# Second MLP of an attention kernel: weights cross DRAM unsplit and are split where they are used

## The chip, the cores and the metric

One core of one Trainium2 chip runs the whole kernel in one launch. The metric is device time in microseconds (us). The engines are TensorE (PE, matmul; PEld is its weight load), VectorE (DVE), ScalarE (ACT), GpSimd (POOL) and SyncE (SP). DMA transfers are issued from the instruction streams of SP and ACT.

## The reference

Linear attention, then two MLPs, each of two layers; 4 x 576 = 2304 tokens, model width 512, hidden width 2048. The weights of the MLPs come as float64, the other inputs and the output as float32.

```python
def phi(x):
    proj = einsum('bhsd,df->bhsf', x, w_phi)
    proj = proj - max(abs(proj), axis=-1)
    return concat([exp(proj), exp(-proj)])
q_p, k_p = phi(q), phi(k)
kv, z = einsum('bhsf,bhsd->bhfd', k_p, v), sum(k_p, axis=2)
x = einsum('bhsf,bhfd->bhsd', q_p, kv) / (einsum('bhsf,bhf->bhs', q_p, z) + 1e-6)
x = x as (2304, 512)
h = x @ moe_w_in;  x = maximum(0.01 * h, h) @ moe_w_out        # first MLP
h = x @ moe2_w_in; out = (h * tanh(softplus(h))) @ moe2_w_out  # second MLP
```

## The kernel before, in words

**Products.** A float32 operand is split in a high part (fp32r, a copy on ACT, `high`) and a low part (the rest, a subtraction on DVE, `low`), and a product is three matmuls: high x high, high x low, low x high (`three`, L95 to L97). Both MLPs work in 2 x 2 blocks with seven products instead of eight. For this each pair f of 128-wide blocks of the hidden width (f = 0 to 7) has seven left operands, A11, A12, A22 and the sums S1 to S4. For the first weights these lie in four parts of a pair: part 0 holds A11 and A12, part 1 A22, part 2 S3 and S1, part 3 S2 and S4. Part 1 is 256 words wide per high or low, the others 512.

**Stages.** The attention comes first, then for each MLP a first layer (`first`: 16 items, one per pair f and half sb of the tokens, and 8 smaller items for the 256 left-over tokens) and a second layer. The first MLP's second layer is `emit_y` in 72 steps. In the second MLP's first layer an item's results leave PSUM by Mish on ACT (`mish`, L1378), differences are formed on DVE (L1402), and seven tiles of 256 KB per item are stored in DRAM (gp<-g, L1376). The second MLP's second layer is `emit_s`: per half 28 steps (7 products x 4 groups of two pairs, fp = 0 to 3), each with 12 matmuls; its inputs are loaded again as 512 KB (raw<-gp, L1430) by `Halves.load` and split (L91, L92) by `Halves.splits`; then 8 steps for the left-over tokens.

**Weights.** A 128-wide block of weights is a unit (MLP, block, 0 for first or 1 for second weights). Its float64 words are loaded (stage<-in_..., 512 KB) and converted (`conversion`, L159) to 128 x 512 float32 words: clamp, shift, sign and mask on DVE, a scale on ACT, a join on DVE. All conversions of the second MLP's weights run during the first MLP. Then:

- First weights, `w2_chain(f)` (L1026), for all eight pairs: the converted words are split in the four parts, the sums formed between, and the split parts stored (pd<-wp). In the second MLP's first layer `load_w2(f, i)` (L1340) loads part i of pair f, 512 or 256 KB in all, straight into the place from which PE reads, when `two_.after` says that pair f-2 is done with that place.
- Second weights: `to_store` writes the converted words (scr<-c). In the second MLP's first layer `o2_chain(f)` (L1275) fetches two units (c<-scr), splits and sums them in the tiles wq ("v4" to "v7"), reordering the columns on the way (`mixed`, `plain`), and stores each of seven operands as high and low (qd<-wq, 256 KB). `to_home(n)` (L1326) loads two pairs of an operand (wo<-qd, 512 KB) into the home from which PE reads, 28 homes in all: 8 behind the gate "s0", 6 behind "s1", 14 behind "c1". These open two steps into the first layer's last cycle, two steps behind that cycle, and at the layer's end.

**Order.** The streams of all engines are written out by hand: `cycle(n)` emits the products of an item (the products that end an item stand in the next item's cycle), and calls `work()` between products, seven times a cycle. `work` advances chains of stages (`Stage`, `Chain`, `Lane`, from L670 on): a queue in order, at most four chains active, the head of the queue not passed by a later one; a stage waits for its gate in `free`, for `after` steps since the stage before, and for tokens that bound DVE's work. `need(mark)` calls `work(True)`, which ignores step counts and tokens, until a stage with that mark is done. `later(n, f)` emits f n steps on. Each DMA of `o2_chain`, `load_w2` and `to_home` is issued by SP, each gp<-g and raw<-gp by ACT.

**Words.** `Places` hands out tiles of 128 x 512 words for converted or fetched weights (`take`, `drop`), the longest unused first. In the second MLP's first layer three are left.

Of the kernel before, what the change touches and what calls it, by code (L numbers as in the profile page):

```python
# [20 lines left out]
def attention_two_mlps_kernel(  # L21
# [17 lines left out]
    P = 128  # L39
# [119 lines left out]
    def conversion(u, then, early=False):  # L159

        box = {}

        def low_bits():
            stg = box["s"]
            e = box["e"] = places.take(places.words) if early else stg[:, :, 0]
            nc.vector.scalar_tensor_tensor(out=e.bitcast(I32) if early else e, in0=stg[:, :, 1], scalar=-(1 << 31),
                                           in1=stg[:, :, 0], op0=ALU.bitwise_and, op1=ALU.bitwise_or)
            if early:
                loaded()
# [5 lines left out]
        def clamp():  # L175
# [3 lines left out]
            nc.vector.tensor_scalar(out=c, in0=stg[:, :, 1].bitcast(F32), scalar1=F64_TOP, scalar2=-F64_TOP,  # L179
                                    op0=ALU.min, op1=ALU.max)  # L180
            nc.vector.tensor_scalar(out=stg[:, :, 0], in0=stg[:, :, 0], scalar1=29, scalar2=None,
# [105 lines left out]
    with tc.manual_schedule():  # L287
# [976 lines left out]
        TO = ((A11,), (A12, A22), (S2, S3), (S4, S1))  # L1264
        qd, home2 = {}, {}

        def mixed(t, *h):

            hs = slice(2 * h[0], 2 * h[0] + 2) if h else slice(0, 4)
            return t.rearrange("p (i x e) -> p x i e", i=KD, x=KD)[:, hs]  # L1270

        def plain(t):
            return t.rearrange("p (x i e) -> p x i e", i=KD, e=P // KD)

        def o2_chain(f):  # L1275
            c, part = [], {}
# [4 lines left out]

            def sums(*todo):
                (l0, r0), (l1, r1) = ([x.rearrange("p (i h y) -> p h i y", i=KD, h=2)[:, h] for h in range(2)] for x in c)
# [4 lines left out]
            def views(i):  # L1288
                if i not in part:
                    part[i] = place("v%d" % (4 + i), F32R, 2, DM, name="wq")  # L1290
                src = mixed(c[i % 2], 0) if i == 0 else mixed(c[i % 2])
                n = E if i == 0 else 2 * E
                return [plain(part[i][:, x, 0:n]) for x in range(2)] + [src]

            def hi(i):
                return lambda: high(views(i))

            def lo(i):
                def put():
                    for x, o in enumerate(TO[i]):  # L1300
                        if (o, f // 2) not in qd:
                            qd[o, f // 2] = dr.tile([P, 2, 2, E], F32, name="qd%d_%d" % (o, f // 2))
                        nc.sync.dma_start(out=qd[o, f // 2][:, f % 2], in_=part[i][:, :, x * E:(x + 1) * E].bitcast(F32))
                return lambda: (low(views(i)), later(2, put))
# [375 lines left out]
```

## Time and profile before

| | |
|---|---|
| time, three runs | 948.32, 949.54, 949.75 us; median 949.54 |
| profiled execution | 947.93 us, span 945.8 us |
| PE busy | 903.7 us (96%) |
| DVE, ACT busy | 626.7 us (66%), 503.6 us (53%) |
| mean granted PE clock | 0.981 of full |
| moved by DMA | 231.88 MB, 245 GB/s over the span |
| chain that ended last | PE 80%, DMA 14%, DVE 3% |

The span runs from the first to the last instruction; the time holds some 2 us around it. The first MLP's first layer begins near 175 us, its second layer near 346, the second MLP's first layer at 543 and its second at 749. A releaser (`<-`) is inferred: it is what ended an engine's idle time.

### The profile page before, as it was taken

To read this page: it belongs to the slowest core of one execution; us is meant where nothing else is said; L and a number is where in the kernel's file an instruction comes from. 1 tells how busy PE (TensorE), PEld (TensorE's weight loads), DVE (VectorE), ACT (ScalarE), POOL (GpSimd) and SP (SyncE) were. 2 spreads that over 40 slices of the span, in tenths; PEclk is the share of its full clock that TensorE was granted. 3 is DMA by queue.
4 is the path that set the end of the run, shared out by engine and by line. 5 is a ranking of instruction groups with operands and counts; after the bars stand their busy time and mean duration, and the time that the engine had idled before them with its cause. 6 is when DMAs were issued, how large, how long until landed. Compare 5 with 4: busy or idle time off the path is not lost.

```text
span 945.8 us, 17104 instructions
## 1 busy us (share of the span) xinstructions
PE 903.7 (96%) x6549; PEld 772.2 (82%) x6549; DVE 626.7 (66%) x1055; ACT 503.6 (53%) x827; POOL 68.7 (7%) x36
## 2 busy tenths in 40 slices
PE   8999999999999999999999998988999569999998
PEld 7999999788888888889888887776778448888887
DVE  7999988588889437888898266545553235654551
ACT  6898898565566554545555264433442234444441
POOL 4435333000000000000000000000000000000000
PEclk9999999999999999999999999998999779999999
DMA  7535420369888777899974639999999996786772
GB/s 208 140 80 159 125 71 8 119 220 327 277 287 268 257 259 248 316 345 328 311 266 153 205 120 315 384 374 367 344 374 367 415 415 219 216 242 209 213 196 59
DMA packets 159554, 231.88 MB, mean 245 GB/s; under 512 B 51569, under 2 KB 91633, under 8 KB 159473
## 3 DMA queue, kind: packets, MB, share of 16 engines
q1 hardware_dynamic: 110336, 127.50, 41.3%
q10 hardware_dynamic: 49136, 103.31, 31.4%
q8 instruction: 51, 0.84, 0.4%
q14 instruction: 31, 0.25, 0.1%
HBM read 136.90 MB, written 93.85 MB: 244 GB/s over the span
## 4 chain that ended last, share of the span: by engine, by line
PE 80%; DMA 14%; DVE 3%; ACT 1%; issue 1%; ACTq 1%; POOL 0%; SPq 0%; DVEq 0%
PE a L95 13%; PE a L96 12%; PE a L97 12%; PE b L95 11%; PE b L96 11%; PE b L97 11%; DMA gp<-g 5%; DMA qd<-wq 4%; PE outs L479 3%; PE kvp L456 3%; DMA w<-pd 2%; DMA wo<-qd 2%; PE a L372 1%; PE xt L504 1%; DMA raw<-gp 1%; PE kvp L459 1%
## 5 line engine op out<-in xcount | busy, mean ns | idle before, releaser
L92 DVE TENSOR_TENSOR g<-raw,g 128x1024 fp32r<-128x1024 f32 (+1 forms) x64 | 76.1, 1189 | 87.2 <-ACT g L91 87.1
L91 ACT ACTIVATE g<-raw 128x1024 fp32r<-128x1024 f32 (+1 forms) x64 | 66.1, 1032 | 94.1 <-PE b L97 40.4
L92 DVE TENSOR_TENSOR gl<-raw,gh 128x512 fp32r<-128x512 f32 x72 | 49.7, 690 | 43.4 <-ACT gh L91 41.5
L91 ACT ACTIVATE gh<-raw 128x512 fp32r<-128x512 f32 x72 | 45.1, 628 | 61.0 <-PE b L97 17.9
L439 POOL PARTITION_ALL_REDUCE qm<-qd x32 | 68.5, 2188 | 86.0 <-ACT qd L434 77.2
L95 PE MATMUL b<-win,w 128*128 128x512 f32 x128 | 51.8, 405 | 18.9 <-ACT b L780 11.1
L96 PE MATMUL b<-gl,wo 128*128 128x512 f32 (+1 forms) x192 | 67.9, 354 | 0.0
L95 PE MATMUL b<-gh,wo 128*128 128x512 f32 (+1 forms) x192 | 67.9, 354 | 0.0
L97 PE MATMUL b<-gh,wo 128*128 128x512 f32 (+1 forms) x192 | 67.9, 354 | 0.0
L1402 DVE TENSOR_TENSOR g<-g,g 128x512 f32<-128x512 f32 x32 | 22.1, 690 | 44.3 <-ACT g L1382 44.0
L96 PE MATMUL b<-win,w 128*128 128x512 f32 x128 | 50.9, 398 | 0.0
L97 PE MATMUL b<-win,w 128*128 128x512 f32 x128 | 50.8, 397 | 0.0
L95 PE MATMUL a<-gh,wo 128*128 128x512 f32 x128 | 49.8, 389 | 0.0
L96 PE MATMUL a<-gl,wo 128*128 128x512 f32 x128 | 49.8, 389 | 0.0
L97 PE MATMUL a<-gh,wo 128*128 128x512 f32 x128 | 49.8, 389 | 0.0
L95 PE MATMUL b<-g,wo 128*128 128x512 f32 x128 | 49.8, 389 | 0.0
L96 PE MATMUL b<-g,wo 128*128 128x512 f32 x128 | 49.8, 389 | 0.0
L97 PE MATMUL b<-g,wo 128*128 128x512 f32 x128 | 49.8, 389 | 0.0
L95 PE MATMUL a<-g,wo 128*128 128x512 f32 x96 | 39.4, 410 | 9.9 <-ACT g L91 9.9
L95 PEld LDWEIGHTS b<-win,w 128*128 128x128 f32 x128 | 24.7, 193 | 26.5 <-ACT b L780 13.7
L830 DVE TENSOR_TENSOR g<-b,z 128x512 f32<-128x512 f32 x31 | 21.3, 689 | 30.6 <-PE b L97 30.1
L95 PE MATMUL a<-win,w 128*128 128x512 f32 x96 | 38.4, 400 | 2.5 <-DMA w<-pd 2.5
(280 smaller groups left out, 2601.0 us busy)
## 6 DMA issues: line engine op xcount, KB each, us to landing
gp<-g ACTq DMA_DIRECT2D x112, 256.0 KB, 5.2
raw<-gp ACTq DMA_DIRECT2D x56, 512.0 KB, 4.3
raw<-gd ACTq DMA_DIRECT2D x72, 256.0 KB, 3.7
gd<-g ACTq DMA_DIRECT2D x71, 256.0 KB, 3.5
stage<-in_moe_w_in_dram SPq DMA_DIRECT2D x32, 512.0 KB, 5.2
stage<-in_moe_w_out_dram SPq DMA_DIRECT2D x32, 512.0 KB, 5.0
qd<-wq SPq DMA_DIRECT2D x56, 256.0 KB, 5.4
wo<-qd SPq DMA_DIRECT2D x28, 512.0 KB, 7.7
```

The lines of the kernel that those rows point to most:

```text
L91: nc.scalar.activation(out=hi, in_=src, func=AF.Copy)
L92: nc.vector.tensor_tensor(out=lo, in0=src, in1=hi.bitcast(F32), op=ALU.subtract)
L95: nc.tensor.matmul(out=o, lhsT=wh_, rhs=xh, start=start, stop=False, **kw)
L96: nc.tensor.matmul(out=o, lhsT=wh_, rhs=xl, start=False, stop=False, **kw)
L97: nc.tensor.matmul(out=o, lhsT=wl_, rhs=xh, start=False, stop=stop, **kw)
L372: nc.tensor.transpose(out=t[:, j * P:(j + 1) * P], in_=s[nm + "n"].rearrange("p h t d -> p (h t d)")[:, j * P:(j + 1) * P], identity=ident)
L439: nc.gpsimd.partition_all_reduce(qm, qd, P, bass_isa.ReduceOp.absmax)
L456: nc.tensor.matmul(out=both[r, h, a, :], lhsT=s["kp"][a][:, h, t, r], rhs=s["vm"][:, h, t, :], start=(a == 0 and h == 0 and t == 0), stop= ...
L459: nc.tensor.matmul(out=both[r, :, a, :], lhsT=l["lp"][a][:, i % 2, r], rhs=s["vl"], start=False, stop=(a == 1), skip_group_check=True)
L479: nc.tensor.matmul(out=g[r, u // 2, u % 2, h], lhsT=s["qp"][a][:, h, q0 + r.start:q0 + r.stop], rhs=s["kv"][:, 2 * h + a], start=(a == 0), ...
L830: nc.vector.tensor_tensor(out=c, in0=x["Y"], in1=cur[0].z7[n % 2], op=ALU.add)
L1402: nc.vector.tensor_tensor(out=out_, in0=in0, in1=in1, op=ALU.subtract)
```

## The change

The second MLP's weights cross DRAM in another form. (1) `conversion`: units of the second MLP's second weights are permuted as they are converted (`mixed`, `flat`), so that later readers find the columns in order. (2) Only pairs 0 and 1 of the first weights go through `w2_chain`; the units of pairs 2 to 7 are stored as plain words. (3) `late_chain(f)` fetches the two units of such a pair in the second MLP's first layer and splits them into the places of `load_w2`, part by part, as pair f-2 leaves them. (4) `o2_chain` stores A11, A12 and A22 straight from the fetched words, forms the sums and stores them, unsplit: 128 KB each. (5) `to_home` loads 256 KB into one of six tiles ("a0" to "a5") and splits them into the home. (6) The two stage tiles "st0" and "st1" give four more words in this stage.

```diff
 def conversion(u, then, early=False):
+        turned = bool(u[0] and u[2])
+        mixed = lambda t: t.rearrange("p (x i e) -> p i x e", x=KD, i=KD)
+        flat = lambda t: t.rearrange("p (i x e) -> p i x e", x=KD, i=KD)
         def low_bits():
+            if turned:
+                nc.vector.tensor_scalar(out=mixed(e.bitcast(I32)), in0=flat(stg[:, :, 0]), scalar1=29, scalar2=None,
+                                        op0=ALU.logical_shift_right)
+                nc.vector.scalar_tensor_tensor(out=e.bitcast(I32), in0=box["c"].bitcast(I32), scalar=-(1 << 31),
+                                               in1=e.bitcast(I32), op0=ALU.bitwise_and, op1=ALU.bitwise_or)
+                return loaded()
...
+            nc.vector.tensor_scalar(out=mixed(c) if turned else c, in0=flat(high) if turned else high, scalar1=F64_TOP, scalar2=-F64_TOP,
                                     op0=ALU.min, op1=ALU.max)
+            if turned:
+                return low_bits()
...
             if u[2] == 0:
-                todo.pop(0)
-                w2_chain(u[1] // 2)
+                v = todo.pop(0)
+                if u[1] // 2 < 2:
+                    w2_chain(u[1] // 2)
+                else:
+                    to_store(u)
+                    to_store(v)
...
         def o2_chain(f):
...
-            chain(Stage(0.0, get, gate="l2", ok=lambda force: places.room(2)),
-                  Stage(0.0, hi(0), gate="v4", after=LAND - 1),
-                  Stage(0.42, both(lo(0), hi(1))),
-                  Stage(0.69, lo(1)),
-                  Stage(0.84, lambda: sums(0, 2)),
-                  Stage(0.84, lambda: sums(2, 4)),
-                  Stage(0.0, hi(2)),
-                  Stage(0.69, both(lo(2), hi(3), lambda: places.drop(c[0]))),
-                  Stage(0.69, both(lo(3), lambda: places.drop(c[1]))),
-                  Stage(0.0, lambda: None, ("o2", f), after=3))
+            chain(Stage(0.0, get, gate="l2", ok=lambda force: places.room(2)),
+                  Stage(0.0, lambda: (put(A11, half(0)[0]), put(A12, half(0)[1]), put(A22, half(1)[1])), after=LAND - 1),
+                  Stage(0.84, lambda: sums(0, 2), after=LAND - 1),
+                  Stage(0.84, lambda: sums(2, 4)),
+                  Stage(0.0, lambda: (put(S1, half(1)[1]), put(S3, half(1)[0]), put(S2, half(0)[0]), put(S4, half(0)[1]))),
+                  Stage(0.0, lambda: [places.drop(x) for x in c], ("o2", f), after=LAND - 1))
+        def late_chain(f):
+            def get():
+                for i in range(2):
+                    c.append(fetch((1, 2 * f + i, 0)))
+                    kept[1, 2 * f + i, 0] = c[i]
+            def p(i):
+                def at():
+                    if i not in part:
+                        part[i] = two_.wt[f, i] = w2_place(f, i)
+                    x = c[i in (1, 2)]
+                    return part[i] + [x[:, E:] if i == 1 else x]
+                return at
...
+            g = lambda i: ("w2", f - 2, i)
+            chain(Stage(0.0, get, gate="l2" if f == 2 else g(0), ok=lambda force: places.room(2)),
+                  Stage(0.0, hi_(p(0)), gate=g(0), after=LAND - 2),
+                  Stage(0.69, both(lo_(p(0)), hi_(p(1))), ("w2", f, 0), gate=g(1)),
+                  Stage(1.27, both(lo_(p(1)), sums[0]), ("w2", f, 1)),
+                  Stage(0.84, both(sums[1], hi_(p(2))), gate=g(2)),
+                  Stage(0.69, both(lo_(p(2)), drop_(1), hi_(p(3))), ("w2", f, 2), gate=g(3)),
+                  Stage(0.69, both(lo_(p(3)), drop_(0)), ("w2", f, 3)))
         for f in range(NF):
+            if f + 2 < NF:
+                late_chain(f + 2)
             o2_chain(f)
...
         def to_home(n):
             o, fp = PHASES[n // 4][0], n % 4
-            def go():
-                t = home2[o, fp] = place(HOMES[n], F32R, 2, 2, E, pool=late[0] if n < 2 * OPS else fix, name="wo2")
-                nc.sync.dma_start(out=t.bitcast(F32), in_=qd[o, fp])
-            return Stage(0.0, go, ("h", o, fp), gate="s0" if n < 8 else "s1" if n < 2 * OPS else "c1")
+            def get():
+                box.append(place("a%d" % (n % 6), F32, 2 * E, name="wr"))
+                nc.sync.dma_start(out=box[0], in_=qd[o, fp].rearrange("p a n -> p (a n)"))
...
+            chain(Stage(0.0, get, gate="s0"),
+                  Stage(0.0, hi_(views), gate="s0" if n < 8 else "s1" if n < 2 * OPS else "c1", after=LAND - 2),
+                  Stage(0.69, lo_(views), ("h", o, fp)))
...
-        two_.after = lambda f, parts: [load_w2(f + 2, i) for i in parts if f + 2 < NF]
+        two_.after = lambda f, parts: free.update(("w2", f, i) for i in parts)
...
+        for x in range(2):
+            t = place("st%d" % x, F32, 2, DM, pool=gp, name="more")
+            places.words += [places.Word(lambda t=t, i=i: t[:, i]) for i in range(2)]
```

## Rows read from the trace of the kernel before

**Rows 1.** The page, part 2: the span in 40 equal slices.
```profile
PE   8999999999999999999999998988999569999998
...
GB/s 208 140 80 159 125 71 8 119 220 327 277 287 268 257 259 248 316 345 328 311 266 153 205 120 315 384 374 367 344 374 367 415 415 219 216 242 209 213 196 59
```

**Rows 2.** Windows: us, busy us and (x instructions) by engine, PEclk, DMA share, GB/s.
```profile
400.00:425.00 25.00, 25.00 (x112) 20.71 (x111) 22.45 (x43) 11.71 (x20) 0.00 (x0) 1.00 0.95 332
585.00:735.00 150.00, 136.27 (x636) 112.22 (x635) 75.58 (x132) 56.82 (x101) 0.00 (x0) 0.97 1.02 370
735.00:748.86 13.86, 6.09 (x25) 5.33 (x24) 4.56 (x6) 4.91 (x7) 0.00 (x0) 0.63 1.03 414
...
800.00:900.00 100.00, 100.00 (x443) 82.80 (x442) 55.13 (x56) 45.75 (x49) 0.00 (x0) 1.00 0.74 219
```

**Rows 3.** Timeline, TensorE: start us, duration us, what; phases' first matmuls.
```profile
543.37 0.39 PE L95 MATMUL a<-win,w 128*128 128x512 f32 x1
...
748.86 0.43 PE L95 MATMUL a<-g,wo 128*128 128x512 f32 x1
...
917.71 0.28 PE L95 MATMUL a<-wo,g 128*128 128x256 f32 x1
...
918.90 0.28 PE L96 MATMUL a<-wo,g 128*128 128x256 f32 x1
```

**Rows 4.** Groups of matmuls, 585 to 735: count, busy, mean ns, idle before.
```profile
L95 PE MATMUL b<-win,w 128*128 128x512 f32 x98 | 39.5, 403 | 11.1 <-ACT b L780 11.1
...
L95 PE MATMUL a<-win,w 128*128 128x512 f32 x71 | 28.7, 404 | 2.5 <-DMA w<-pd 2.5
```

**Rows 5.** Waits of TensorE, 500 to 780: us in total, times, longest.
```profile
PE a L95 <- ACT g L91: 9.9, 2, 6.7
PE b L95 <- DVE g L830: 7.8, 1, 7.8
```

**Rows 6.** DMA, 585 to 735: count, KB each, median us to landing.
```profile
DMA packets 34427, 55.43 MB, mean 370 GB/s; under 512 B 3103, under 2 KB 16621, under 8 KB 34416
...
gp<-g ACTq DMA_DIRECT2D x82, 256.0 KB, 5.2
qd<-wq SPq DMA_DIRECT2D x49, 256.0 KB, 5.4
wo<-qd SPq DMA_DIRECT2D x11, 512.0 KB, 7.6
w<-pd SPq DMA_DIRECT2D x20, 256.0 KB, 5.7
w<-pd SPq DMA_DIRECT2D x9, 512.0 KB, 6.7
c<-scr SPq DMA_DIRECT2D x12, 256.0 KB, 5.4
```

**Rows 7.** DMA, 540 to 580.
```profile
gp<-g ACTq DMA_DIRECT2D x16, 256.0 KB, 2.1
...
c<-scr SPq DMA_DIRECT2D x4, 256.0 KB, 3.1
```

**Rows 8.** DMA, 735 to 780.
```profile
raw<-gp ACTq DMA_DIRECT2D x9, 512.0 KB, 8.2
gp<-g ACTq DMA_DIRECT2D x12, 256.0 KB, 7.5
```

**Rows 9.** Timeline of the transition: start us, duration us, what, idle before.
```profile
715.36 27.83 SPq L1331 DMA_DIRECT2D wo<-qd  x16
...
760.11 1.06 ACT L91 ACTIVATE g<-raw 128x1024 fp32r<-128x1024 f32 x1 [5.04 <-DMA gp<-g]
```

**Rows 10.** Groups of split and conversion instructions, whole span, ACT and DVE.
```profile
L250 ACT ACTIVATE wq<-c 128x512 fp32r<-128x512 f32 x24 | 15.1, 627 | 14.7 <-DMA w<-pd 5.3 <-issue 3.1 <-DVE g L1402 2.1
...
L254 DVE TENSOR_TENSOR wq<-c,wq 128x512 fp32r<-128x512 f32 x24 | 16.5, 686 | 7.4 <-ACT wq L250 7.2
...
L181 DVE TENSOR_SCALAR stage<-stage 128x512 int32<-128x512 int32 x64 | 27.0, 422 | 0.0
```

More of the change, by code (lines that the diff above doesn't have):

```diff
@@ L1263, in attention_two_mlps_kernel, with put, half, sums @@
               row(1.22, lo_(b_(T4)), mark=("x2", 1, T4)))
-        TO = ((A11,), (A12, A22), (S2, S3), (S4, S1))
         qd, home2 = {}, {}
[L1267 to L1273, printed above, removed]
-        def o2_chain(f):
+        def o2_chain(f):
+            c = []
+            def get():
+                for i in range(2):
+                    c.append(fetch((1, 2 * f + i, 1)))
+            def put(o, t):
+                if (o, f // 2) not in qd:
+                    qd[o, f // 2] = dr.tile([P, 2, E], F32, name="qd%d_%d" % (o, f // 2))
+                nc.sync.dma_start(out=qd[o, f // 2][:, f % 2], in_=t)
+            def half(i):
+                return [x[:, i * E:(i + 1) * E] for x in c]
+            def sums(*todo):
+                (l0, l1), (r0, r1) = half(0), half(1)
+                for o, x, op, y in ((r1, r0, ALU.add, r1), (r0, l0, ALU.subtract, r0),
+                                    (l0, r1, ALU.subtract, l0), (l1, l1, ALU.subtract, l0))[slice(*todo)]:
+                    nc.vector.tensor_tensor(out=o, in0=x, in1=y, op=op)
+            chain(Stage(0.0, get, gate="l2", ok=lambda force: places.room(2)),
[5 more added lines that the diff above has]
+        def late_chain(f):
             c, part = [], {}
@@ L1279, in get @@
                 for i in range(2):
-                    c.append(fetch((1, 2 * f + i, 1)))
-            def sums(*todo):
-                (l0, r0), (l1, r1) = ([x.rearrange("p (i h y) -> p h i y", i=KD, h=2)[:, h] for h in range(2)] for x in c)
-                for o, x, op, y in ((r1, r0, ALU.add, r1), (r0, l0, ALU.subtract, r0),
-                                    (l0, r1, ALU.subtract, l0), (l1, l1, ALU.subtract, l0))[slice(*todo)]:
-                    nc.vector.tensor_tensor(out=o, in0=x, in1=y, op=op)
@@ L1288, in views @@
[L1288 to L1304, printed above, removed]
@@ L1317, in attention_two_mlps_kernel @@
-        chain(Stage(0.0, lambda: free.add("v4"), gate="l2",
-                    ok=lambda force: not any(("x2", 1, o) in undone for o in range(OPS))))
+                    c.append(fetch((1, 2 * f + i, 0)))
[7 more added lines that the diff above has]
+                return at
@@ new lines, in late_chain @@
+            sums = [lambda: w_sums(f, slice(0, 2), 1), lambda: w_sums(f, slice(2, 4), 1)]
+            g = lambda i: ("w2", f - 2, i)
+            drop_ = lambda i: (lambda: places.drop(c[i]))
+            chain(Stage(0.0, get, gate="l2" if f == 2 else g(0), ok=lambda force: places.room(2)),
[5 more added lines that the diff above has]
+                  Stage(0.69, both(lo_(p(3)), drop_(0)), ("w2", f, 3)))
@@ L1448, in w_home @@
             need("h", o, f // 2)
-            return [home2[o, f // 2][:, f % 2, x] for x in range(2)]
+            return [home2[o, f // 2][:, x, f % 2 * E:(f % 2 + 1) * E] for x in range(2)]
         def emit_s(s, i):
@@ L1524, in attention_two_mlps_kernel, with natural, apart @@
         left_out = {}
+        def natural(t, *h):
+            return t.rearrange("p (i x e) -> p x i e", i=KD, x=KD)[:, slice(2 * h[0], 2 * h[0] + 2) if h else slice(0, KD)]
+        def apart(t):
+            return t.rearrange("p (x i e) -> p x i e", i=KD, e=P // KD)
         def finish_left(t, h=None, eng=None):
@@ L1530, in finish_left @@
             if h is None:
-                nc.scalar.activation(out=mixed(o), in_=plain(sum_of[t]), func=AF.Copy)
+                nc.scalar.activation(out=natural(o), in_=apart(sum_of[t]), func=AF.Copy)
             elif h == 0:
-                nc.vector.tensor_copy(out=mixed(o, h), in_=plain(sum_of[t][:, 0:E]))
+                nc.vector.tensor_copy(out=natural(o, h), in_=apart(sum_of[t][:, 0:E]))
             else:
-                nc.scalar.activation(out=mixed(o, h), in_=plain(sum_of[t][:, E:]), func=AF.Copy)
+                nc.scalar.activation(out=natural(o, h), in_=apart(sum_of[t][:, E:]), func=AF.Copy)
             if h == 0:
@@ L1604, in attention_two_mlps_kernel @@
         cur[0] = two_
+        for x in range(2):
+            t = place("st%d" % x, F32, 2, DM, pool=gp, name="more")
+            places.words += [places.Word(lambda t=t, i=i: t[:, i]) for i in range(2)]
         rate[0] = 1.42
```

22 lines of the change are left out of this document (13 added, 9 removed).

## The prediction, made before the changed kernel ran

> **What bounds the kernel now.** I read the page's 40 slices first: PE shows 9 nearly everywhere, with three 8s, a 5 and a 6 from slice 25 to 33, where the line of GB/s stands between 315 and 415 [rows 1]. So matmul is the bound except in the second MLP's first layer and the entry to its second layer. Each matmul of 512 columns takes 100 us / 443 = 0.2257 us where nothing disturbs it [rows 2]; one of 256 columns takes (918.90 - 917.71) / 10 = 0.119 us [rows 3].
>
> The code gives the work. The second MLP's first layer is 16 items of 7 products of 6 matmuls (672 of 512 columns) and 8 left items of 24 matmuls of 256 columns: 672 x 0.2257 + 192 x 0.119 = 174.5 us. It runs from 543.37 to 748.86 [rows 3], 205.5 us, so 31.0 us are lost. The part of the second layer with two halves is 56 steps of 12 matmuls, again 672, 151.7 us; it runs from 748.86 to 917.71 [rows 3], 168.9 us, so 17.2 us are lost. Together **48.2 us**. From 543 to 585 and behind 780 next to nothing is lost, by the slices; between 585 and 735 I count 636 matmuls [rows 2], 509 of them of 512 columns by shape (six groups: 98 x 3 + 72 + 72 + 71, the first and the last in [rows 4]): 509 x 0.2257 + 127 x 0.119 = 130.0 of 150 us, a loss of 20.0. That leaves 11.0 for the last cycle (735 to 748.86) and 17.2 for the entry to layer two. Part of the loss is clock and not idle time: of its two levels, 2.4 and 1.2 GHz, PE is granted a mean of 0.97 in 585 to 735 and 0.63 in the last cycle [rows 2], where it sat idle 7.8 us in one piece [rows 5].
>
> The waits of PE name ACT and DVE, which copy out sums (L780, 11.1 us [rows 4], and L830 [rows 5]) and split (L91, 9.9 us [rows 5]). Neither is full: 57 and 76 us of 150 [rows 2]. What is full is DMA: its share is 1.02 at 370 GB/s, and 1.03 at 414 in the last cycle [rows 2]; the same store gp<-g that lands in 2.1 us at 540 to 580 takes 5.2 here and 7.5 at the transition [rows 6 to 8]. ACT and DVE stand behind stores whose tile has not come free: at 760.11 ACT had sat idle 5.04 us for gp<-g [rows 9]. DMA is the cause, ACT the messenger. At 400 to 425 the first MLP moves 332 GB/s, share 0.95, with PE busy all 25 us [rows 2]; I take that as a load that this kernel bears.
>
> **The change part by part.**
>
> *Bytes, steady part.* In 585 to 735 the core moves 55.43 MB. Of it w<-pd is 20 x 256 + 9 x 512 KB = 9.96 MB, qd<-wq 49 x 256 KB = 12.85 MB, wo<-qd 11 x 512 KB = 5.77 MB [rows 6]. A pair's split first weights are 3 x 512 + 256 KB = 1.835 MB, its plain words 0.524 MB: 9.96 becomes 2.85. The sums halve: 12.85 becomes 6.4, 5.77 becomes 2.9. So 55.4 - 7.1 - 6.4 - 2.9 = 39.0 MB; over the 130 us that PE needs this is 300 GB/s, below the 332 that it bears. The steady loss of 20.0 us goes, but for what is late next.
>
> *Late next: the split weights.* Pairs 2 to 7 now need fetch, high part on ACT and low part on DVE, with a copy and a subtraction of 0.63 and 0.69 us [rows 10] for 512 columns. A pair takes 3 full parts and a half part, 2.3 us ACT and 2.5 us DVE, and four subtractions of 256 columns, bounded by half and all of 0.69, 1.4 to 2.8 us. A pair lasts 14 x 1.354 + 24 x 0.119 = 21.8 us. ACT is at 57/150 and loses as much from the old wq splits as it gains; DVE rises from 50% by at most 5.3/21.8 less the old 2.5, to about 65%. Neither becomes the bound. In time: the place of pair f comes free when f-2 was last used, and from pair 3 on that is two cycles ahead (19 us), against about 6 work steps of 1.354 us for fetch, wait and the first split. Only pair 2 is tight: its third part is split one step before the product that reads it, so I charge 1 us. The fetch is given 4 steps, 5.4 us, before ACT asks; it lands in 3.1 us at low load [rows 7] and 5.4 in the saturated part [rows 6], so ACT waits little if the load falls. Steady remainder: **2 us**, bounds 0 and 8 (half a step of 1.354 us on each of 12 gates).
>
> *The lane.* late_chain(f+2) stands in the queue ahead of o2_chain(f) and doesn't start until its gate, so o2 chains now come one per pair. By step counts chains 5, 6 and 7 run in cycles 12 to 14; the last one's puts leave one or two steps before `need("o2", 7)`. One forced step, no stall. Seven words instead of three hold them.
>
> *Homes.* Before, 16 loads of 512 KB are issued in one run of 27.83 us from 715.36 [rows 9]. Now 28 loads of 256 KB, four chains at a time, each four steps of waiting and one or two of splitting: some 0.7 per step, 0.18 MB per 1.354 us, 136 GB/s. With gp<-g, one of 256 KB a step (194 GB/s), that is 330 GB/s in the last cycle. The first eight homes are split before layer two starts, the rest come at 0.7 a step where 0.5 is used up. Their split adds 28 x 0.63 to ACT and 28 x 0.69 to DVE [rows 10], in a stretch where these have 46 and 55 us in 100 [rows 2]. The last cycle's 11.0 us shrink to **2**, bounds 0 and 6: ACT now issues the first three raw loads into tiles that held words, and may wait for the last puts (one landing less the two steps between).
>
> *Entry to layer two.* Here load stays high: the last 12 gp<-g and 9 raw<-gp [rows 8] fall in some 18 us of work, with about 8 homes: 3.1 + 4.7 + 2.1 MB, 550 GB/s if all were needed at once, though some of it may come later. The fourth raw load is issued in step 0, lands perhaps 5 to 7 us later (8.2 before [rows 8]), then is split; step 3 starts 8.1 us after step 0. The fifth needs the tile of the last T3 store. I expect 2 to 4 us of idle in steps 3 and 4, and some time at the lower clock after. Of 17.2 us **6** stay, bounds 2 and 14.
>
> *Conversion, first MLP.* The second weights are now permuted when converted. Two tensor_scalars of 0.42 us [rows 10] write in 32-word blocks; at worst they cost 0.69, the subtraction row. So 16 units x 2 x 0.27 = 8.6 us of DVE at most, and no gain, as number and size of the operations stay. The splits of six pairs leave the same engine in that stretch, 6 x 2.5 us. PE is busy all the time there, so I cost it at 0; without that cover it is the 8.6.
>
> *Sum.* 48.2 - 2 - 2 - 6 = 38.2, less 0.8 because one matmul record more or less in the 443 moves the pitch by 0.2%: 37.4 off. The profiled execution took 947.9 us (span 945.8 and 2.1 around it): 910.5. The median of the runs, 949.5, stands 1.6 above that execution; carried over, **912 us**. With no remainder at all it would be 901, with all upper bounds (8 + 6 + 14) 929.
>
> **The rivals.**
>
> *A, the entry stays bound by DMA.* For it: at the transition the demand worked out above is over the 414 GB/s that were moved there [rows 2]. Against it: half of the homes' bytes are gone and their run is paced. Then the 17.2 and half of the 11.0 stay, and the gain is 20 - 2 + 5.5 = 23.5: 924 us.
>
> *B, transfers count and not bytes.* The number of puts and homes is unchanged; in 585 to 735 there are 29 w<-pd [rows 6], of which some 11 fetches remain, so of about 196 transfers 178 are left, 9% less instead of 30%. 55.43 x 0.91 = 50.4 MB-equivalents at 370 GB/s is 136 us, 6 over PE's 130; the transition stays whole. Gain 14: 934 us. Against: the 128 KB of each put lie in rows as long as before, in half the number.
> The Trainium skill, DMA: Bandwidth & Descriptors, section Anatomy of one DMA, gives each transfer (there one issued by GpSimd) a fixed cost of about 2.0 us beside its bytes over 436 GB/s; as an estimate by that page a put falls from 2.6 to 2.3 us and not to a half, which is this rival. The trace speaks half for it: at low load 256 KB land in 2.1 us [rows 7], so little of that can be bytes; but the 414 GB/s of the transition [rows 2] show the fixed part overlapped when many are in flight.
>
> *C, slower.* ACT's stream now holds 52 high splits that each follow a load of fixed lead, 24 for weights and 28 for homes; behind each stand the copies that free PE's banks. If loads land later than the lead of 5.4 us by enough, PE waits at each. To lose the 48.2 won, 52 waits must cost 0.93 us each beyond PE's cover, about 6.5 us of landing. The transition's 7.5 to 8.2 [rows 8] is beyond that point, the steady 5.4 isn't, and bytes fall. If it holds throughout at 8 us, 52 x 1.7 = 88 lost less 48: 988; nearer its edge, 955.
>
> *D, no change*: the stall isn't DMA but ACT's and DVE's own work; their 38% and 50% [rows 2] speak against it. 948.
>
> **How the numbers follow.** Forecast 0.72 (901 to 922), A 0.15, B 0.08, C 0.03, D 0.02. The range 903 to 927 leaves out B, C, D and the tips of the forecast and of A, in all just under 0.2. A measurement here can tell 0.2%, 2 us, from no change: faster 0.95, same 0.02, slower 0.03.
>
> **What would show it.** Right: in the first layer DMA share under 0.95 and some 300 GB/s, gp<-g landing under 4 us, PE 10 tenths and clock 1.00; waits of PE on L780 and L830 gone; what is left of idle stands at the first steps of layer two, on L91 behind raw<-gp. Wrong: ACT's high splits waiting for c<-scr or the homes' loads with PE idle behind them (C), landing times unchanged at fewer bytes (B), or a gap as long as before at the entry (A).

## The result: 923.1 us, and the profile after

| | before | after |
|---|---|---|
| median, 4 runs each | 949.64 us (948.32 to 951.28) | 923.12 us (922.25 to 923.56) |
| ratio | | 0.9719, 95% interval 0.9702 to 0.9736 |
| profiled execution, span | 947.93, 945.8 us | 922.25, 920.1 us |
| moved by DMA | 231.88 MB | 201.47 MB |

2.8% faster; the range of 903 to 927 held the time, the forecast of 912 lay 11 us too low, and the time lies just outside the 901 to 922 that the forecast itself was given. Times after the table are read from one profiled execution each. The kernel after has other line numbers: L780, L830 and L835 are L792, L842 and L847; gp<-g is L1405, Mish L1411, the T differences L1431, raw<-gp L1459, the sums L1301, their stores L1292, the homes' loads L1352, the homes' and weights' splits L262 (ACT) and L266 (DVE).

First the marks of the phases on TensorE (start us, duration us, what, and in brackets the idle time before and what ended it), which answer to [rows 3]:

```profile
544.90 0.39 PE L95 MATMUL a<-win,w 128*128 128x512 f32 x1
...
725.03 0.80 PE L95 MATMUL b<-win,w 128*128 128x512 f32 x1 [5.68 <-DVE g L842]
...
730.24 0.39 PE L95 MATMUL a<-g,wo 128*128 128x512 f32 x1
...
737.38 0.50 PE L95 MATMUL a<-g,wo 128*128 128x512 f32 x1 [1.53 <-ACT g L91]
738.63 0.50 PE L96 MATMUL a<-g,wo 128*128 128x512 f32 x1 [0.76 <-DVE g L92]
...
743.81 0.79 PE L95 MATMUL a<-g,wo 128*128 128x512 f32 x1 [2.39 <-ACT g L91]
745.07 0.80 PE L96 MATMUL a<-g,wo 128*128 128x512 f32 x1 [0.47 <-DVE g L92]
...
891.74 0.28 PE L95 MATMUL a<-wo,g 128*128 128x256 f32 x1
```

The first layer of the second MLP took 730.24 - 544.90 = 185.3 us, 10.8 more than the 174.5 that its matmuls need; the two-half part of the second layer 161.5, 9.8 more than 151.7. Before these were 31.0 and 17.2. The 25.7 us between the two profiled executions are 20.2 + 7.3, less 1.5 by which the first layer starts later and 0.3 behind 891.74. The windows (us, busy us and instructions by engine, granted clock, DMA share, GB/s) tell where the 10.8 lie; they answer to [rows 2]:

```profile
545.00:605.00 60.00, 60.00 (x294) 50.86 (x293) 41.21 (x65) 31.29 (x51) 0.00 (x0) 1.00 0.58 210
605.00:615.00 10.00, 10.00 (x52) 8.55 (x51) 4.04 (x7) 3.03 (x6) 0.00 (x0) 1.00 1.05 358
615.00:690.00 75.00, 75.00 (x366) 63.44 (x364) 46.08 (x86) 34.09 (x60) 0.00 (x0) 1.00 0.79 279
...
690.00:705.00 15.00, 14.05 (x73) 11.57 (x72) 11.05 (x23) 5.22 (x9) 0.00 (x0) 1.00 0.89 308
705.00:720.00 15.00, 14.35 (x69) 11.80 (x67) 4.16 (x6) 5.65 (x10) 0.00 (x0) 1.00 0.99 348
720.00:735.00 15.00, 9.97 (x39) 8.58 (x40) 11.39 (x17) 6.52 (x12) 0.00 (x0) 0.77 0.67 240
735.00:750.00 15.00, 9.86 (x29) 6.70 (x28) 9.23 (x13) 7.98 (x11) 0.00 (x0) 0.79 1.02 383
```

From 545 to 690 TensorE was never without work, at full clock: the steady loss is gone. The 10.8 stands in the last forty us before the layer's end, and the 9.8 in the first twenty of the next: by counting matmuls as the prediction did, 0.7 us are lost up to 690, 1.9 from there to 717.75, and 8.3 behind that, in the last cycle. In both stretches the granted clock fell behind a piece of idle time, to 0.50 (the lower of its two levels, 1.2 GHz) from 725 to 730 and from 745 to 750, so that the piece cost more than its length: the matmuls at 725.03 and 743.81 take 0.80 and 0.79 us. The transfers of 585 to 700 (count, KB each, median us to landing), against [rows 6]:

```profile
DMA packets 20487, 31.48 MB, mean 274 GB/s; under 512 B 2269, under 2 KB 8068, under 8 KB 20478
...
gp<-g ACTq DMA_DIRECT2D x74, 256.0 KB, 2.4
qd<-more SPq DMA_DIRECT2D x24, 128.0 KB, 3.1
more<-scr SPq DMA_DIRECT2D x12, 256.0 KB, 4.5
```

gp<-g, which took 5.2 us to land, takes 2.4. What is late at the end of the layer is seen on VectorE and ScalarE:

```profile
717.97 2.19 ACT L262 ACTIVATE wo<-wr 128x512 fp32r<-128x512 f32 x4 [0.68 <-ACT g L1411]
720.07 1.06 ACT L1411 ACTIVATE g<-b 128x512 f32<-128x512 f32 x2
```
```profile
720.67 0.69 DVE L1431 TENSOR_TENSOR g<-g,g 128x512 f32<-128x512 f32 x1 [6.79 <-ACT g L1411]
721.28 1.89 DVE L266 TENSOR_TENSOR wo<-wr,wo 128x512 fp32r<-128x512 f32 x3
723.09 0.68 DVE L1431 TENSOR_TENSOR g<-g,g 128x512 f32<-128x512 f32 x1
723.69 0.68 DVE L266 TENSOR_TENSOR wo<-wr,wo 128x512 fp32r<-128x512 f32 x1
724.29 0.68 DVE L842 TENSOR_TENSOR g<-b,z 128x512 f32<-128x512 f32 x1
```

L842 frees the bank for the matmul at 725.03. Ahead of it in DVE's stream stand four low splits of homes and two differences, and the first difference waited 6.79 us for a Mish that stands in ACT's stream behind four high splits of homes in one burst. ACT had also been late before: 2.17 us up to 710.19 and 2.50 up to 715.65, both ended by a home's load. No instruction of ACT reads that load there; a store of ACT stood behind it, as run 11 explains.

### The profile page after: what moved, and what is told of

The parts are those of the page before. It is cut to its first block, busy times and chain, and to the rows that moved or that the text cites. A ratio compares the mean times of both kernels' runs of the same rounds, so it can differ in the third digit from the quotient of the medians.

```text
span 920.1 us, 17012 instructions
## 1 busy us (share of the span) xinstructions
PE 898.2 (98%) x6549; PEld 770.8 (84%) x6549; DVE 624.7 (68%) x1051; ACT 504.2 (55%) x823; POOL 68.7 (7%) x36
## 2 busy tenths in 40 slices
DMA packets 148353, 201.47 MB, mean 219 GB/s; under 512 B 51120, under 2 KB 84528, under 8 KB 148272
## 4 chain that ended last, share of the span: by engine, by line
PE 89%; DVE 4%; DMA 3%; ACT 1%; issue 1%; ACTq 1%; POOL 0%; SPq 0%; DVEq 0%
PE a L95 14%; PE a L96 14%; PE a L97 13%; PE b L95 13%; PE b L96 13%; PE b L97 13%; PE outs L491 3%; PE kvp L468 3%; PE a L384 1%; DMA wr<-qd 1%; PE xt L516 1%; PE kvp L471 1%; DVE g L1431 1%; DMA gp<-g 1%; DMA raw<-gp 1%
## 5 line engine op out<-in xcount | busy, mean ns | idle before, releaser
L91 ACT ACTIVATE g<-raw 128x1024 fp32r<-128x1024 f32 (+1 forms) x64 | 66.0, 1032 | 71.7 <-PE b L97 33.8
L91 ACT ACTIVATE gh<-raw 128x512 fp32r<-128x512 f32 x72 | 45.1, 628 | 70.8 <-PE b L97 23.7
L95 PE MATMUL b<-win,w 128*128 128x512 f32 x128 | 50.8, 397 | 6.6 <-DVE g L842 6.4
L96 PE MATMUL b<-win,w 128*128 128x512 f32 x128 | 50.3, 393 | 0.0
L97 PE MATMUL b<-win,w 128*128 128x512 f32 x128 | 50.3, 393 | 0.0
L842 DVE TENSOR_TENSOR g<-b,z 128x512 f32<-128x512 f32 x31 | 21.4, 689 | 41.8 <-PE b L97 41.7
L96 PEld LDWEIGHTS b<-gl,wo 128*128 128x128 f32 x192 | 36.3, 189 | 5.0
L95 PEld LDWEIGHTS b<-gh,wo 128*128 128x128 f32 x192 | 36.3, 189 | 5.0
L97 PEld LDWEIGHTS b<-gh,wo 128*128 128x128 f32 x192 | 36.3, 189 | 5.0
```

Source lines behind the costliest of these rows:

```text
L91: nc.scalar.activation(out=hi, in_=src, func=AF.Copy)
L95: nc.tensor.matmul(out=o, lhsT=wh_, rhs=xh, start=start, stop=False, **kw)
L96: nc.tensor.matmul(out=o, lhsT=wh_, rhs=xl, start=False, stop=False, **kw)
L97: nc.tensor.matmul(out=o, lhsT=wl_, rhs=xh, start=False, stop=stop, **kw)
L842: nc.vector.tensor_tensor(out=c, in0=x["Y"], in1=cur[0].z7[n % 2], op=ALU.add)
```

## The experiments

Theory: layer one's remaining 10.8 us and the entry's 9.8 come from what was put into the last cycle, the homes' loads and splits and the last sums, in that order on SP, ACT and DVE; the steady part got free because fewer bytes move. Rivals: each of the two edits brings its part on its own account; the number of transfers counts and not their bytes.

Each run's profiled execution, split as above (what the first layer lost over 174.5 us and the second's two halves over 151.7), and the ratio of its time to the kernel before's, measured beside it. Where a wait sits at the border of the layers, the sum of the two is the figure to read. One profile can lie off its run's median: run 5's execution took 914.5 us, 4 under the median, run 4's 933.7, while another of its four took 927.6.

| run | median us | ratio, 95% | layer one | layer two |
|---|---|---|---|---|
| before | 949.64 | | 31.0 | 17.2 |
| after | 923.12 | 0.9719 (0.9702 to 0.9736) | 10.8 | 9.8 |
| 1 splits later | 919.41 | 0.9685 (0.9661 to 0.9710) | 4.7 | 13.1 |
| 2 loads later too | 915.09 | 0.9644 (0.9621 to 0.9667) | 12.2 | 3.0 |
| 3 first weights only | 948.69 | 0.9988 (0.9973 to 1.0003) | 28.6 | 19.0 |
| 4 sums only | 932.87 | 0.9817 (0.9782 to 0.9852) | 21.4 | 11.3 |
| 5 sums spread | 918.52 | 0.9650 (0.9624 to 0.9677) | 4.4 | 9.9 |
| 6 first homes early | 915.78 | 0.9629 (0.9611 to 0.9648) | 5.9 | 8.7 |
| 7 first weights, own lane | 939.53 | 0.9881 (0.9859 to 0.9903) | 21.5 | 19.3 |
| 8 each sum stored 3 times | 949.46 | 0.9986 (0.9972 to 0.9999) | 38.6 | 8.6 |
| 9 entry's loads ahead | 912.26 | 0.9591 (0.9569 to 0.9613) | 4.2 | 6.2 |
| 10 extra stores, SP | 935.63 | 0.9840 (0.9821 to 0.9860) | 24.7 | 9.3 |
| 11 stores in halves | 938.28 | 0.9869 (0.9846 to 0.9892) | 25.8 | 10.0 |
| 12 extra stores, GpSimd | 943.46 | 0.9924 (0.9903 to 0.9944) | 32.4 | 10.5 |

**1 and 2: the homes out of the last cycle.** Run 1 lets the first eight homes' high splits wait for "s1", behind the last cycle; run 2 lets all homes' loads wait for it too.

```diff
-            chain(Stage(0.0, get, gate="s0"),
-                  Stage(0.0, hi_(views), gate="s0" if n < 8 else "s1" if n < 2 * OPS else "c1", after=LAND - 2),
+            chain(Stage(0.0, get, gate="s1"),          # run 1: "s0" as after
+                  Stage(0.0, hi_(views), gate="s1" if n < 2 * OPS else "c1", after=LAND - 2),
```

> The high splits of the first eight homes wait for gate s1 instead of s0, so that they and their low splits stand behind the last cycle's copies; the loads stay where they are. Theory T (splits stand ahead of the copy L842 that PE's last cycle waits for): the 5.7 us wait of PE on L842 falls under 2 us, and with the lower clock behind it 3 to 6 us go: 917 to 920 us. Rival R (DMA load of homes and raw tiles holds ACT in that cycle, splits or not): the gap stays at 4 us or more, 922 to 924 us.

> As e1, and the loads of the homes wait for s1 too, so that none of them is under way in the last cycle. T: no better than e1 in the last cycle, and worse at the entry to layer two, where the first home lands late by 2 to 4 us: 919 to 924 us. R: only here does the last cycle's gap close, and ACT's idle time before 716 us (2.2 and 2.5 us) with it: 914 to 918 us, clearly under e1.

PE's waits in run 1 from 545 to 765 (us in total, times, longest):

```profile
PE a L97 <- DVE wo L266: 5.3, 1, 5.3
PE b L95 <- DVE g L842: 1.9, 2, 1.0
PE a L95 <- ACT g L91: 1.7, 2, 1.4
```

The wait for L842 shrank from 6.4 to 1.9 us, and layer one's loss by 6.1: the burst of splits did hold L842 up. But the first step of layer two then waited 5.3 us for a home's own low split. In run 2 the same wait is 6.1 us, ended by the home's high split and ahead of the first matmul of layer two, so that it counts in layer one's 12.2; behind it layer two loses only 3.0. The two together are 20.6 us after, 17.8 in run 1, 15.2 in run 2: what the move saves in the last cycle comes back in part as a first home that is late. Run 2 did not do what its expectation says: a gate sets the place in the stream, and SP, with nothing ahead of the loads, issued the first at 706.24 (705.27 after), before the last cycle. ACT's waits up to 711.30 and 717.07 stayed, 2.28 and 2.22 us, both ended by a home's load. So its 915.1 us, the rival's number, came from splits that stand still later in ACT's stream; a last cycle without homes' loads was not tested here.

**3, 4 and 7: one edit at a time.** Run 3 is the kernel before with first weights as plain words and `late_chain`; run 4 the kernel after with first weights split before they cross DRAM (`w2_chain` and `load_w2` for all pairs). In run 3 `late_chain` at the queue's head held the `o2_chain`s back; run 7 gives it a lane of its own and lets a chain of sums begin when the one before has split its words.

```diff
 run 7, to run 3:
-        main, = lanes = Lane(4),
+        main, side = lanes = Lane(4), Lane(2)
...
-            chain(Stage(0.0, get, gate="l2" if f == 2 else g(0), ok=lambda force: places.room(2)),
+            side.queue.append(Chain([Stage(0.0, get, gate="l2" if f == 2 else g(0), ok=lambda force: places.room(2)),
```

> The first half of the change alone on the kernel before: plain words for pairs 2 to 7 with late splits; sums and homes cross DRAM split as before. By bytes: 55.4 - 7.1 = 48.3 MB over 130 us is 371 GB/s, just at what DMA gave, so of the 20 us lost in the steady part 3 to 8 stay, and the 28 us at the transition stay whole: 932 to 938 us. If transfers counted and not bytes: 18 of 196 fewer, 940 us or more. If ACT's late splits cost something, it shows here too.

> The second half of the change alone: sums cross DRAM unsplit and homes are split where used; the first weights cross split for all pairs as before. By bytes: 55.4 - 6.4 - 2.9 = 46.1 MB over 130 us is 355 GB/s, under the 370 that DMA gave, so 1 to 5 of the steady 20 us stay, and the transition loses what it loses in the changed kernel (20 us): 924 to 928 us. If transfers counted and not bytes, the steady part gains nothing here (their number is as before): 940 us.

> The first half of the change alone as in e3, but late_chain stands in a lane of its own and the chains of sums follow each other as in the kernel before. Theory Q (in e3 late_chain at the head of the queue held the sums back to the last cycles, which gave the gain back): the steady gain shows, 932 to 938 us. Rival S (ACT's splits of the sums wait for the stores of their shared tiles, in whatever order): 944 us or more, as e3.

Windows of runs 3, 4 and 7, each from its own profile:

```profile
585.00:700.00 115.00, 106.56 (x504) 88.13 (x503) 76.54 (x142) 55.88 (x103) 0.00 (x0) 0.99 0.82 291
```
```profile
585.00:700.00 115.00, 105.97 (x492) 88.04 (x492) 46.64 (x79) 36.05 (x61) 0.00 (x0) 0.96 0.88 302
```
```profile
585.00:700.00 115.00, 108.61 (x506) 90.44 (x505) 83.30 (x158) 59.39 (x109) 0.00 (x0) 0.97 0.95 330
```

Runs 3 and 4 missed what was expected of them: at 291 and 302 GB/s, the rate at which the prediction saw no loss, 8 and 9 of 115 us are lost. Run 7 moves more in that stretch, 330 GB/s, and loses less. So the mean rate doesn't decide; what stands late in a stream has a part, and run 11 shows another. With the order mended (run 7) the first weights gain 9.5 us in layer one, the sums (run 4) 9.6, together 19.1 of the 20.2. Run 4 loads its split parts in 50 transfers (540 to 750) where the kernel before has 34, which run 11 shows to cost something; its share is rather too small than too large. The entry is the sums' alone: 17.2 to 11.3 in run 4, no gain in runs 3 and 7.

**5, 6 and 9: spreading the sums, the homes and the raw loads.** Run 5 changes only the queue's order, so that the last two sums' chains no longer come together at the end:

```diff
-        for f in range(NF):
-            if f + 2 < NF:
-                late_chain(f + 2)
-            o2_chain(f)
+        late_chain(2); o2_chain(0); o2_chain(1)
+        for f in range(2, NF):
+            o2_chain(f)
+            if f + 1 < NF:
+                late_chain(f + 1)
```

Run 6 adds to it that A11's four homes are fetched into words and split during the layer, in tiles ("v4" to "v7") idle since its second cycle, and that other homes wait for "s1". Run 9 makes two homes early instead of four and uses "v6" and "v7" for the first two raw loads, issued a cycle earlier, lets five raw loads and not three be under way by then, and ties home n (n > 7) to step n - 8:

```diff
 run 9, to run 6:
-        RAW3 = [("cc", gp), ("st0", gp), ("st1", gp), ("x1_0", fix), ("x1_1", fix)]
+        RAW3 = [("v6", fix), ("v7", fix), ("cc", gp), ("st0", gp), ("st1", gp)]
...
+            if n == len(it) - 2:
+                later(3, lambda: s3.load(0))
+                later(6, lambda: s3.load(1))
...
-            chain(Stage(0.0, get, gate="s1"),
+            chain(Stage(0.0, get, gate="s1" if n < 8 else ("hs", n - 8)),
```

> The changed kernel with the queue reordered: o2_chain 0 to 2 ahead of late_chain 3, so that one chain of sums and not three runs in cycles 12 to 14. If the bunched sums load DMA and DVE ahead of the last cycle, ACT's idle time before 716 us shrinks: 917 to 921 us. Rival: PE was full in those cycles, so their load is paid by nothing: 922 to 924 us.

> As e5, and the four homes of A11 get tiles v4 to v7 (the first splits of layer two take s0 to s3), are fetched into words and split before the last cycle; all other homes are loaded from s1 on. Theory T+R (homes' splits and loads in the last cycle cost it, and the first step waits for its home where they are put later): the 5.7 us wait on L842 and the 6.1 us wait of e2 both go; the wait for raw tiles at steps 3 and 4 stays: 906 to 911 us. Rival (the entry is bound by DMA whatever the order, since 24 homes and the raw tiles now come together): 913 us or more.

> The sums' order and early homes of the run before (915.8 us), with the entry's loads ahead of it: the first two 512 KB raw loads of layer two go out two cycles early into two tiles free since cycle 2, two homes instead of four are made early, and each later home waits for the step eight steps ahead of its own, so that homes no longer run far ahead of need (16 issues in 25 us) and hold up the raw loads (5 to 6 us each at 400 GB/s). Theory, the entry is bound by the order in which transfers are asked for: PE's idle time and half clock between 720 and 750 shrink by 4 to 7 us; 908 to 912 us. Rival, the entry is bound by the sum of its bytes whatever their order, or by the splits behind them on ScalarE and VectorE: 914 to 917. Third, homes asked for only eight steps ahead come late: over 917, with PE waits on the homes' splits.

Run 5 took 6.4 of layer one's 10.8 us away (by its profile; by the medians the whole kernel gained 4.6) and nothing from the entry: SP reached the homes' loads at 694.10 instead of 705.27, for the sums' stores and fetches ahead of them were done. Run 6 stands 2.7 us lower by the medians, but its ratio's interval overlaps run 5's and its two losses add up to no less (14.6 and 14.3): no gain is shown, and 915.8 us is what its rival gave. Of the two waits for L91 at the entry the longer was still 2.9 us. Run 9 brought the entry from 8.7 to 6.2 and layer one to 4.2; 912.3 us, at the upper end of what the theory gave. Its remaining wait (PE, ACT and DVE of run 9, in three fences; gp<-g is L1413 there, Mish L1420, the differences L1440) is no longer a transfer:

```profile
730.61 0.50 PE L95 MATMUL a<-g,wo 128*128 128x512 f32 x1 [2.46 <-ACT g L91]
731.87 0.60 PE L96 MATMUL a<-g,wo 128*128 128x512 f32 x1 [0.76 <-DVE g L92]
```
```profile
722.60 3.04 ACTq L1413 DMA_DIRECT2D gp<-g  x4
725.69 0.60 ACT L1420 ACTIVATE left<-a 128x512 f32<-128x512 f32 x1 [2.87 <-DMA gp<-g]
...
727.42 0.63 ACT L262 ACTIVATE wo<-wr 128x512 fp32r<-128x512 f32 x1 [1.13 <-DVE g L1440]
...
729.51 1.99 ACT L91 ACTIVATE g<-raw 128x1024 fp32r<-128x1024 f32 x2
```
```profile
730.59 1.23 DVE L92 TENSOR_TENSOR g<-raw,g 128x1024 fp32r<-128x1024 f32 x1 [1.22 <-ACT g L91]
```

The raw words that L91 reads had been asked for before 716 and L91 waits for nothing: it stands in ACT's stream behind four high splits of homes, and these behind four stores that took 3.04 us to leave, each 0.33 to 0.39 for its issue and the rest waits for differences on DVE. This is the fastest version here, 1.3% under the kernel after (0.9591 / 0.9719 = 0.987).

**8, 10, 11 and 12: bytes or transfers.** Run 8 stores each sum three times. Run 10 adds stores out of a tile that lies idle. Run 11 cuts each sum's store in two halves of 64 partitions. Run 12 is run 10 with the extra stores issued by GpSimd. The extra stores' data are not used.

```diff
 run 10 (run 12: nc.gpsimd for nc.sync):
+        def extra(n, x):
+            nc.sync.dma_start(out=dr.tile([P, MAIN], F32, name="ex%d_%d" % (n, x)), in_=yt["v4"][:, x % 2])
...
+            if 3 <= n <= 14:
+                for x in range(4):
+                    later(2 * x + 1, lambda n=n, x=x: extra(n, x))
 run 11:
-                nc.sync.dma_start(out=qd[o, f // 2][:, f % 2], in_=t)
+                for x in range(2):
+                    h = slice(x * P // 2, (x + 1) * P // 2)
+                    nc.sync.dma_start(out=qd[o, f // 2][h, f % 2], in_=t[h])
```

> The changed kernel with each sum stored three times (two copies that nobody reads): 12.8 MB more in the first layer, no work for ACT or DVE. If bytes are what bound the steady part: 39 + 12.8 = 52 MB over 130 us is 399 GB/s, more than the 370 that DMA gave, so 8 to 15 us of the steady loss come back: 931 to 940 us, gp<-g landing at 5 us again. Rival (the gain came from ACT and DVE no longer waiting for tiles, not from bytes): 922 to 926 us.

> The changed kernel with four extra 256 KB stores in each of cycles 3 to 14 of the second MLP's first layer, evenly placed, out of a tile that nothing writes or waits for by then; their data goes to scratch and is not used. The demand in the steady part goes from 274 to some 360 GB/s, near the 370 of before, and no engine has more work. Theory, bytes: transfers land in 4 to 5 us again instead of 2.4, and the steady part (585 to 735 us before) gives back 6 to 20 us: 929 to 943 us. Rival, what was lost before lay in how transfers and splits depended on each other and not in the rate: under 927 us, PE between 585 and 700 within 2 us of full.

> The changed kernel with each sum's 128 KB store cut into two 64 KB stores of 64 partitions: 56 more transfers, no more bytes. Theory, bytes: 921 to 925 us. Rival, the number of transfers is what costs: 56 transfers more give back a good part of what the change's fewer transfers gained, over 927 us.

> The extra stores of the run that came to 935.6 us (four of 256 KB in each of cycles 3 to 14, out of an idle tile), issued from GpSimd, which has nothing else to do in this part, instead of SyncE. Two runs gave back 12 to 15 us: that one, with more bytes and more issues on SyncE, and the one with the sums' stores cut in two, with the same bytes and 56 more issues on SyncE, each 0.45 to 0.6 us in its order ahead of the next fetch. Theory, bytes: transfers land later whoever asks for them, and this run stays at 932 to 938 us. Rival, SyncE's order: fetches are asked for too late because SyncE is still issuing stores; without the extra issues there, 922 to 927 us. Between the two, 928 to 931, both have a part.

Run 8 lost the whole gain, more than expected, and can't be read as bytes alone: the sums are formed in place, and DVE waited up to 14.5 us for one of the extra stores to have read its words. In run 10 DVE waited so for 1.8 us at most; its time came out as the theory had it, though gp<-g landed in 3.3 us and not in 4 to 5. Run 11 was the surprise: no byte more, and 15 us given back. Run 10's and run 11's windows, and two of run 11's transfers (against 4.5 us for more<-scr and 3.1 for the whole store after):

```profile
585.00:700.00 115.00, 107.90 (x506) 87.17 (x506) 65.14 (x122) 47.11 (x84) 0.00 (x0) 1.00 0.88 318
```
```profile
585.00:700.00 115.00, 109.12 (x518) 89.59 (x517) 67.23 (x124) 48.08 (x85) 0.00 (x0) 1.00 0.75 252
```
```profile
more<-scr SPq DMA_DIRECT2D x12, 256.0 KB, 4.5
qd<-more SPq DMA_DIRECT2D x32, 64.0 KB, 2.9
```

Landing times are the same and the rate is lower; a store of half the size lands hardly sooner. The Trainium skill (DMA: Bandwidth & Descriptors, section Anatomy of one DMA, for transfers issued by GpSimd) has a transfer's time mostly fixed, so that 64 KB less would save 0.15 us, as an estimate by it; the 3.1 and 2.9 of this trace agree.

What the halves add shows in ACT's stream. The traces name the semaphore that each transfer counts up when it lands. All transfers of SP and ACT take the same eight in turn, and none is issued before the one eight places ahead of it has landed, so that in each of the 14 traces at most eight are under way. A store of ACT can thus stand behind a transfer of SP, and with it the copies and Mishes behind it in ACT's stream. From 545 to 690 ACT stood for such a landing 9.9 us in 16 issues after, 26.4 in 29 in run 11, 28.5 and 25.1 in runs 10 and 8, 33.8 in 41 before; also 33.1 in run 4, but 3.2 in run 3, whose loss is one of order. The same place in the kernel after (ACT, DVE) and in run 11 (ACT, DVE, PE; L1407 is gp<-g, L1433 a difference):

```profile
613.65 0.33 ACTq L1405 DMA_DIRECT2D gp<-g  x1
617.24 0.69 DVE L1431 TENSOR_TENSOR g<-g,g 128x512 f32<-128x512 f32 x1 [2.52 <-ACT g L1411]
```
```profile
616.89 0.33 ACTq L1407 DMA_DIRECT2D gp<-g  x1
620.36 0.69 DVE L1433 TENSOR_TENSOR g<-g,g 128x512 f32<-128x512 f32 x1 [4.78 <-ACT g L1413]
626.76 0.50 PE L95 MATMUL b<-win,w 128*128 128x512 f32 x1 [1.16 <-DVE g L842]
```

After, the store leaves when its Mish ends. In run 11 it leaves 2.41 us later, 0.08 us behind the landing of a fetch of SP (c<-scr), the first difference waits 4.78 and not 2.52 us, and L842 behind it is late for PE. The same comes back at 640.77 and 664.00. Near the layer's end DVE waited 7.60 us, up to 717.27, for a half store to have read its words, as in run 8, and PE then 3.29 us for L847. How the 15.2 us divide between these is open, and so is whether SP's own issue time has a part. 112, 48 and 56 transfers more in runs 8, 10 and 11 cost 26.3, 12.5 and 15.2 us, 0.23 to 0.27 us each, though they added 14.7, 12.6 and 0 MB.

Run 12 was to take SP out of it and did so otherwise than meant, at 943.5 us over the 932 to 938 expected: nothing paces GpSimd, so all 48 stores left between 551 and 598 instead of over twelve cycles. That makes it a test within one run:

```profile
545.00:605.00 60.00, 47.05 (x215) 38.08 (x214) 27.96 (x41) 21.39 (x33) 25.97 (x48) 0.91 0.95 345
605.00:615.00 10.00, 7.67 (x28) 5.85 (x27) 3.29 (x5) 4.15 (x8) 0.00 (x0) 0.83 0.55 207
615.00:690.00 75.00, 75.00 (x367) 63.55 (x366) 48.97 (x92) 34.19 (x60) 0.00 (x0) 1.00 0.74 265
```
```profile
ex<-y POOLq DMA_DIRECT2D x48, 256.0 KB, 8.6
gp<-g ACTq DMA_DIRECT2D x18, 256.0 KB, 8.2
```

While the extra stores run, gp<-g takes 8.2 us and TensorE has work for 47.05 of 60 us, where the kernel after has 60.00; from 615 on, when they are through, it is full again. SP issues nothing more here than after, and GpSimd's stores count up eight semaphores of their own. So bytes in flight do cost, by landing times, and a place among the eight costs beside them. By these rows landing goes by the rate and not by the number: in run 8 180 transfers in 115 us (585 to 700) move 305 GB/s and gp<-g lands in 2.7 us, here 84 in 60 us move 345. The Trainium skill (DMA: Bandwidth & Descriptors, section Issuing engines are not separate DMA queues) says that transfers of all issuers share the same 16 DMA engines; stores of GpSimd that slow ACT's agree.

## Why the prediction was right, and where it failed

- *The steady part, 20.0 us to 2.* Right: nothing is lost from 545 to 690, gp<-g lands in 2.4 us (forecast under 4), the rate is 274 GB/s (300). But the reason given, a load below the 332 GB/s that the first MLP bears, is not what decides: runs 3, 4 and 11 lose 6 to 9 us of 115 at 291, 302 and 252. The steady part got free because its transfers are few (run 11), small (run 12) and asked for in good time (run 3 against run 7), all three. The prediction had ACT stand behind stores whose tile had not come free; the trace of before shows another wait beside it: ACT stood 33.8 and SP 34.5 us, from 545 to 690, for a place among the eight transfers, and 9.9 and 2.3 after.
- *The split weights.* Right that neither ACT nor DVE becomes the bound, and for the weights rival C is out: no wait of PE from 540 to 770 names a split of theirs.
- *The lane.* "One forced step, no stall" was wrong. With `late_chain` at the queue's head the sums came one per pair and bunched behind 690; run 5, which changes that order alone, is 4.6 us faster than the kernel after.
- *Homes.* The step that failed: "The last cycle's 11.0 us shrink to 2, bounds 0 and 6". The loss in the last cycle was 8.3, with 1.9 more just ahead of it. The prediction added up GB/s and busy time for the homes and didn't place them in the streams: four high splits in one burst ahead of a Mish, four low splits ahead of L842 (run 1 moves 6.1 us by moving them), and their loads behind bunched sums on SP (run 5), with ACT's stores behind those loads in turn. It is rival C's picture, copies behind high splits, but by a burst and not by late loads. The saturated DMA that caused the loss before was replaced by the order of work on ACT and DVE.
- *The entry, 17.2 to 6, bounds 2 and 14.* 9.8, within bounds, in part by the mechanism named: the fourth raw load is split at 742.71, when it has landed, as step 3 waits. But it was issued at 737.12, as step 2 waited, and not in step 0; and what step 2 waited for, 1.53 us, was no landing but ACT, which reached the third raw split at 736.27 though its load had gone out at 713.84. Runs 3, 4 and 7 show that the sums' part of the change brought this (their halved bytes and paced loads together), run 9 that 3.6 of the remaining 9.8 go with issue order.
- *The rivals.* A's number, 924, is the measured one (counted from the profiled execution; from the median, as the 912, A gives 926), but not by A's sum: it kept the whole entry and half of the last cycle, and three quarters of the last cycle stayed and little over half of the entry. So that the time lies in the range is in part luck: the range reached up to it for A's sake. B as stated is out: run 7, with as many transfers of sums and homes as after but twice their bytes, loses 16.4 us more, and gp<-g lands in 3.7 us there with 146 transfers from 585 to 700, in 2.4 after with 145 (run 7 also splits its sums elsewhere, so not all of the 16.4 need be bytes). Yet the number that B counted has a price of its own (run 11). The forecast gave it none.
- *The sum.* 6.3 us too little for the last cycle, 0.5 for what lies ahead of it, 3.8 for the entry, and 1.8 for a later start of the layer and the end of the kernel, less the 0.8 set aside: 11.6, against 922.25 - 910.5 = 11.75 of the profiled executions.

What stays open: how run 11's price divides, for 64-partition stores may also be dearer to the DMA engines (share 0.75 at 252 GB/s against 0.77 at 274); and whether eight places cost something that more would give back, for no run changes their number. That the layer starts 1.5 us later after the change need not be the change: in the runs with the same conversion it starts at 543.8 to 545.7, so the permuted conversion, costed at 0, shows no price beyond that.

## What to carry to other kernels

When a saturated resource is relieved, price what was moved into each in-order stream at the place where it stands, not its sum over a stage: here the gain of the steady part was whole, while 8.3 of the last cycle's 11.0 us stayed until the queue was reordered. A transfer has two prices, its bytes for whoever shares the DMA engines and its place among the eight under way for whoever issues next, on either queue; halving the bytes of each transfer and keeping their number saves one of them. Here the order of chains and idle tiles, which let first loads and splits go out early, were worth 11 us more (923 to 912) without a byte less.

## What was not expected of the hardware

- Two engines that issue transfers can hold each other up: in these traces SP and ACT never have more than eight under way together, and a store of ACT left 0.08 us behind the landing of a fetch of SP (run 11, 616.89). Whether the eight are the chip's or the way these programs use their semaphores is not shown.
- An issue can take longer when much is under way: on ACT mostly 0.33 us, but of the four raw<-gp from 737.12 after the change three took 0.80, 0.49 and 0.49 us, at 396 GB/s from 736 to 742.
- A half of a store lands hardly sooner than the whole (2.9 against 3.1 us), so cutting a transfer bought nothing and cost a place more, some 0.27 us of the kernel's time each (15.2 / 56).
